# Windowed attention feeding a two-layer ELU network on one core: another order of the first weight and value loads, and of the last pair of the second tile

## The chip, the cores and the metric

The kernel runs on one core of one Trainium2 chip. The metric is the device time of one execution in microseconds. Three runs of the kernel before gave 301.75, 302.62 and 303.54 us; the median is 302.62 us.

## What is computed

There are 8 batches with 8 heads of 576 rows and 64 columns, so 4608 tokens of 512 values. Attention looks at a window of 32 rows on each side; its output goes through two dense layers with an ELU between them.

```python
# _attn_ref, for every batch and head
scores = 1/sqrt(D) * q @ k.T, kept where |i - j| <= 32
x = softmax(scores) @ v                      # [4608, 512] after the heads are put side by side
# _moe_ref
h = x @ w_in                                 # [4608, 2048]
g = np.where(h > 0.0, h, np.exp(np.minimum(h, 0.0)) - 1.0)
out = g @ w_out                              # [4608, 512]
```

Inputs and output are float32; inside the kernel the operands of the matmuls are bf16.

## The kernel before

**Attention by pairs.** A pair is two blocks of 64 query rows with all 8 heads, 128 tokens; there are 36. For pair i, `scores(i)` (L372) are 16 small matmuls into a PSUM tile, `exponential(i)` (L393) is one ScalarE instruction, `mask(i)` a VectorE product (pairs 0 to 3 get their band added in PSUM instead), `pv(i)` (L409) 16 matmuls against the values, `normalize(i)` (L423) a reciprocal and a product on VectorE that make `x_st`. `x_transpose(i)` (L434) turns `x_st` by four TensorE transposes into a PSUM bank, and `x_evac(i)` (L451) copies it into half of `xT[t]`, the moving operand of tile t. The PSUM tiles of pairs 2 and 3 are "s" and "u".

**Values in two layouts.** Even blocks read `V_e`, odd ones `V_o`, the same rows shifted by 64. For batch 0 the loads bring `V_o` (`load_v_odd`, L157), and `rotate_back` (L163) copies its halves into `V_e` on VectorE. `pv(3)` needs `load_v_odd(0, 3)` and half of the copy made from it.

**The dense layers by tiles and steps.** A tile is 256 tokens (two pairs); there are 18. A step is 256 columns of the middle layer, 8 for a tile. `mm1(kk)` (L703) is the first layer for step `order[kk]`: 8 matmuls of 256 columns for TensorE (`products`, L729), four for each half j of the step. Then comes `exponents(kk)` (L747), the exponential on ScalarE, and behind it `subtract(kk)` (L756), which takes 1 away, on ScalarE for kk 1, 3 and 4 and on VectorE otherwise. `elu(kk)` (L766) is one VectorE instruction that reads the PSUM tile and makes `g_sb`. `mm2(n)` (L820) adds step n to the output sums with 4 matmuls of 512 columns.

**The order of the start.** `order` begins with tile 0 steps 0 and 1 (kk 0, 1), tile 1 steps 0 and 1 (kk 2, 3), then tile 0 steps 2 and 3 (kk 4, 5), and so on. Steps kk 2 and 3 are made by pairs (`BY_PAIRS`, L727): first both with pair 2's 128 columns, then both with pair 3's, 8 matmuls of 128 columns each time, in the PSUM tiles "s" and "u". Every other `mm1` takes the tile "h0" or "h1", by the parity of kk, so `mm1(8)` waits until `elu(6)` has read "h0".

**What sets the order of the work.** The schedule is written out by hand: each engine runs its instructions in the order in which the program issues them. `at(kk, slot, fn, ...)` (L569) puts a call into step kk: "dve" ahead of `mm1`, "half" between the halves j of `mm1`, "mid" behind `mm1`, a number n ahead of `mm2(n)`, "end" at the end of the step. All loads with a cast to bf16 are issued on GpSimd's queue in program order (L488 to L502 and L547 to L557): values, weights, and the cast groups `load_cast` (L138) of queries and keys. `load_w_in(c, z, nz)` (L197) loads part z of nz of quarter c of w_in, which is two steps wide; half a quarter is one step, a quarter of it (a sixteenth of w_in) half a step. `load_w_out` (L205) does the same for the rows of w_out. The quarter 3 of w_in is first needed by `mm1(12)`.

**The cast groups.** `transpose_casts` (L595) runs `elu(8)`, then turns the queries and keys of batch 1's first part and of batch 0's last rows on TensorE: 38 transposes into two PSUM tiles, `pk` and `pt`. ScalarE evicts `pk`, VectorE `pt` with three copies. Pair 4 (`scores(4)` at the end of step 9) needs them, and takes the PSUM tile "s" that `pt` had.

Of the kernel before, what the change touches and what calls it, by code (L numbers as in the profile page):

```python
# [10 lines left out]
BF16 = mybir.dt.bfloat16  # L11
# [10 lines left out]
def kernel(  # L22
# [9 lines left out]
    nc = tc.nc  # L32
# [61 lines left out]
    def ps_tile(shape, dt, tag, name):  # L94
        return pools[tag].tile(shape, dt, tag=tag, name=name)
# [42 lines left out]
    def load_cast(b, which, part):  # L138
        z, nj = part
        mj = nj if nj < 3 else HJ + 1  # L140
        t = cpool.tile([128, 2, mj * D], BF16, tag=f"c{which}{mj}",
                       name=f"c{which}")[:, :, 0:nj * D]
        qk_c[b, which, z] = t
        src = (q, k)[which][b, :, z:z + NC * nj, :].rearrange(
            "(g h) (c j) d -> c g h (j d)", h=2, j=nj)
        nc.gpsimd.dma_start(out=t, in_=src)  # L146
# [10 lines left out]
    def load_v_odd(b, m):  # L157
        lo = 128 * m + WIN
        nc.gpsimd.dma_start(  # L159
            out=V_o[b % 3][:, m, :, 0:D],  # L160
            in_=v[b, :, lo:lo + 128, :].rearrange("h p d -> p h d"))

    def rotate_back(b, m0, m1, parts=(0, 1)):  # L163
        e, o = V_e[b % 3], V_o[b % 3]
        for z in parts:
            nc.vector.tensor_copy(e[64 * (1 - z):64 * (2 - z),
                                    m0 + z:m1 + z],
                                  o[64 * z:64 * (z + 1), m0:m1])
# [28 lines left out]
    def load_w_in(c, z=0, nz=1):  # L197
        w = D_FF // 4 // nz
        c = c * nz + z
        nc.gpsimd.dma_start(  # L200
            out=w_in_sb[:, :, c * w:(c + 1) * w],
            in_=moe_w_in[:, c * w:(c + 1) * w].rearrange(
                "(o p) f -> p o f", p=128))

    def load_w_out(c, z=0, nz=1):  # L205
        n = NFO // 4 // nz
        c = c * nz + z
        nc.gpsimd.dma_start(
            out=w_out_sb[:, c * n:(c + 1) * n, :],
            in_=moe_w_out[c * n * 128:(c + 1) * n * 128, :].rearrange(  # L210
                "(o p) f -> p o f", p=128))
# [51 lines left out]
    def make_masks():  # L263
        nc.gpsimd.affine_select(
            out=masks, in_=masks, compare_op=ALU.is_ge, fill=0.0,
            base=0, pattern=[[0, 5], [-1, QB]], channel_multiplier=1)
        nc.gpsimd.affine_select(
            out=masks, in_=masks, compare_op=ALU.is_ge, fill=0.0,
            base=2 * WIN, pattern=[[0, 5], [1, QB]], channel_multiplier=-1)
        for mi in (0, 4):  # L270
            nc.gpsimd.affine_select(
                out=masks[:, mi, :], in_=masks[:, mi, :],
                compare_op=ALU.is_ge, fill=0.0, base=-WIN,
                pattern=[[0, QB]], channel_multiplier=1)
        nc.gpsimd.affine_select(
            out=masks[:, 3, :], in_=masks[:, 3, :], compare_op=ALU.is_ge,
            fill=0.0, base=128 - WIN - 1, pattern=[[0, QB]],
            channel_multiplier=-1)
# [209 lines left out]
    for which in range(2):  # L488
        load_cast(0, which, FRONT_B[which])
    load_w_in(0, 0, 2)  # L490
    for m in (2, 3):
        load_v_odd(0, m)
    for z in (2, 3):
        load_w_in(0, z, 4)
    load_w_in(1)
    load_w_out(0, 0, 2)
    load_w_out(0, 1, 2)
    load_v(0, 4, HIGH)
    for which in range(2):
        load_cast(0, which, FRONT_C[which])  # L500
    load_w_out(1)
    make_masks()  # L502

    idle(10, "y1")
# [37 lines left out]
    scores(3)  # L542
    exponential(3)
    rotate_back(0, 2, 3)
    rotate_back(0, 3, 4, (0,))

    load_w_in(2, 0, 2)  # L547
    for which in range(2):
        load_cast(1, which, ONE_A)
    load_w_in(2, 1, 2)  # L550
# [18 lines left out]
    def at(kk, slot, fn, *args):  # L569
        tasks.setdefault((kk, slot), []).append((fn, args))  # L570

    def run(kk, slot):
        for fn, args in tasks.get((kk, slot), ()):
            fn(*args)
# [7 lines left out]
        at(kk + 2, "end", x_evac, i, nc.scalar)  # L582


    for i in (2, 3):
        at(0, ("half", "mid")[i - 2], pv, i)
        at(0, ("half", "mid")[i - 2], normalize, i)
    at(1, "half", x_transpose, 2, "y0")
    at(1, "half", x_evac, 2, nc.scalar)
    at(1, "mid", x_transpose, 3, "y1")  # L590
    at(1, "mid", x_evac, 3, nc.vector)
    at(5, "dve", swap_pools)


    def transpose_casts():  # L595
        elu(8)
        n, (nq, nk) = ONE_A[1], (c[1] for c in FRONT_C)
        pk = ps_tile([128, 1024], BF16, "h1", "ptx")
        pt = ps_tile([128, 2048], BF16, "s", "ptx")
        first, then = [], []  # L600
        transpose_qk(1, 1, ONE_A, 0, n, nc.scalar, later=first, pt=pk)
        for b, which, part, lo in ((1, 0, ONE_A, 0), (0, 0, FRONT_C[0], n),
                                   (0, 1, FRONT_C[1], n + nq)):
            transpose_qk(b, which, part, 0, part[1], nc.vector, later=then,
                         pt=pt[:, lo * 128:(lo + part[1]) * 128])
        for evict in first + then:
            evict()

    at(8, 6, transpose_casts)
    at(6, "dve", rotate_back, 0, 3, 4, (1,))  # L610

    for which in range(2):
# [18 lines left out]
    for i in range(4, NPAIR):  # L631
        two = i >= FIRST_TWO
        kk, z = begin[i], i % 2 if two else 0
# [69 lines left out]
    def mm1(kk):  # L703
        t, s = order[kk]
        if kk == BY_PAIRS[1]:
            return
        ks = BY_PAIRS if kk == BY_PAIRS[0] else (kk,)
        tags = ((f"h{kk % 2}", "s") if kk == NSTEP - 1 else
                ("s",) if kk == 2 else ("u",) if kk == 3 else (f"h{kk % 2}",))
        for k in ks:  # L710
            psH[k] = []
        for z, tag in enumerate(tags):
            for k in ks:
                psH[k].append(ps_tile([128, FG // len(tags), TT], FP32,
                                      tag if k == kk else "u", "ps"))
        for p in range(len(ks)):
            for k in ks:
                for z in range(len(tags)):
                    products(k, z, p if len(ks) > 1 else None)
                if p == len(ks) - 1:  # L720
                    for z in range(len(tags)):
                        exponents(k, z)
                        if k == NSTEP - 1:
                            elu(k, z)
# [4 lines left out]
    def products(kk, z, pair):  # L729
        t, s = order[kk]  # L730
        ps = psH[kk][z]
        w = ps.shape[1]
        for j in range(w):
            fo = s * FG + z * w + j
            for do in range(NDO):
                if pair is None:
                    o, r = ps[:, j, :], xT[t][:, :, do, :]
                else:
                    o = ps[:, j, pair * 128:(pair + 1) * 128]
                    r = xT[t][:, pair, do, :]  # L740
                nc.tensor.matmul(  # L741
                    o, lhsT=w_in_sb[:, do, fo * 128:(fo + 1) * 128],
                    rhs=r, start=(do == 0), stop=(do == NDO - 1))
            if j == 0 and pair is None:
                run(kk, "half")

    def exponents(kk, z):  # L747
        ps = psH[kk][z]
        e_sb = mpool.tile([128, ps.shape[1], TT], FP32, tag="e_sb",
                          name="e_sb")  # L750
        nc.scalar.activation(e_sb, ps, AX.Exp)  # L751
        e_t[kk, z] = e_sb
        if kk > 0:
            subtract(kk, z)
# [11 lines left out]
    def elu(kk, z=0):  # L766
        if z == 0:
            g_t[kk] = mpool.tile([128, FG, TT], BF16, tag="g_sb", name="g_sb",
                                   bufs=8)
        if kk == 0:  # L770
            subtract(kk, z)
        ps = psH[kk][z]
        w = ps.shape[1]
        nc.vector.scalar_tensor_tensor(  # L774
            g_t[kk][:, z * w:(z + 1) * w, :], ps, 0.0, m_t.pop((kk, z)),
            ALU.max, ALU.min)
# [70 lines left out]
    for kk in range(NSTEP):  # L847
        run(kk, "first")
        for n in {1: (), 2: (0, 1), 9: ()}.get(kk, (kk - 1,)):
            if n >= 0:  # L850
                elu(n)
        run(kk, "dve")
        mm1(kk)
        run(kk, "mid")
        if kk == NSTEP - 1:
            last_sums()
        elif kk >= LATE + LAG:
            for _ in range(3 if kk < LATE + LAG + 4 else 4):
                add(*todo.pop(0))
        else:  # L860
            for n in {2: (), 3: (), 4: (), 5: (0, 2), 6: (1, 3), 7: (4,),
                      8: (5, 6)}.get(kk, (kk - LAG,) if kk >= LAG else ()):
                run(kk, n)
                mm2(n)
        run(kk, "end")
# [30 lines left out]
```

## Time and profile before

| what | value |
|---|---|
| median of three runs | 302.62 us |
| the profiled execution's own time | 302.36 us |
| its span in the profile | 300.6 us |
| time around the span (302.36 - 300.6) | 1.76 us |
| TensorE (PE) busy | 293.7 us, 98% of the span |
| VectorE (DVE) busy | 242.1 us, 81% |
| ScalarE (ACT) busy | 169.0 us, 56% |
| GpSimd (POOL) busy | 52.3 us, 17% |
| granted TensorE clock | 1.0 |

Times in the profile count from the start of the span. In a line of the timeline the first number is the start, the second the length, both in us; what stands in brackets at the end is how long the engine had been idle and what ended that. Consecutive matmuls overlap in the records, so the distance between their starts, not their length, says what one costs. A load has a time of issue on its queue and a time to landing.

The loads at the start, all on GpSimd's queue, with the trace's own times:

| load | issued us | landed us |
|---|---|---|
| values for pair 2 (`load_v_odd(0, 2)`, 128 KB) | 7.15 | 14.60 |
| values for pair 3 (`load_v_odd(0, 3)`, 128 KB) | 8.02 | 15.56 |
| w_in third sixteenth (128 KB) | 8.88 | 17.00 |
| w_in fourth sixteenth (128 KB) | 9.63 | 17.40 |
| w_in quarter 1 (512 KB) | 10.41 | 19.92 |
| w_out, two halves of quarter 0 (256 KB each) | 11.14, 12.25 | 21.18, 23.03 |
| w_out quarter 1 (512 KB) | 17.29 | 26.26 |
| w_in, first half of quarter 2 (256 KB) | 19.79 | 27.60 |
| cast group of batch 1, queries and keys (256 KB each) | 20.55, 21.71 | 28.93, 30.20 |
| w_in, second half of quarter 2 (256 KB) | 23.32 | 31.50 |
| w_in quarter 3 (512 KB) | 27.89 | 38.95 |

### The profile page before, as it was taken

The page shows a single profiled execution, that of the slowest core. Times are in us where ns is not written, and L with a number is a line of the kernel's source. Part 1 is how long each engine was busy: PE and PEld are TensorE (multiplying, and loading weights), DVE is VectorE, ACT ScalarE, POOL GpSimd, SP SyncE. Part 2 cuts the span into 40 slices and gives each one's busy share as a digit, 9 for nine tenths or more (in the row PEclk, how much of TensorE's full clock was granted, in tenths as well). Part 3 has the DMA queues.
Part 4 walks back from the last instruction along what each step waited for, and adds up shares of the span by engine and source line. Part 5 has one row for each costly group of instructions (what it writes and reads, how often), then busy time and mean ns, then how long its engine had stood idle before and what let it go on. Part 6 is the DMA issues. An engine that isn't in the chain of part 4 may idle for free.

```text
span 300.6 us, 7712 instructions
## 1 busy us (share of the span) xinstructions
PE 293.7 (98%) x3116; PEld 198.1 (66%) x3116; DVE 242.1 (81%) x481; ACT 169.0 (56%) x256; POOL 52.3 (17%) x74
## 2 busy tenths in 40 slices
PE   6999999999999999999999999999999999999995
PEld 2575667677666666666666666666666666666673
DVE  6787787988787988887889789887988787877673
ACT  3873458688655567456745665467535353534332
POOL 8777204520005000410032002300000000000000
PEclk9999999999999999999999999999999999999999
DMA  9999999999967969999699989997921121111011
GB/s 190 167 198 202 187 232 338 372 190 171 290 181 209 234 115 260 236 280 140 158 264 326 161 203 253 310 155 141 271 47 72 35 72 38 70 37 70 2 70 71
DMA packets 94069, 52.74 MB, mean 175 GB/s; under 512 B 78162, under 2 KB 83794, under 8 KB 94034
## 3 DMA queue, kind: packets, MB, share of 16 engines
q0 software_dynamic: 44976, 10.03, 45.3%
q1 hardware_dynamic: 47330, 35.74, 44.7%
q10 hardware_dynamic: 1728, 6.49, 5.9%
q8 instruction: 24, 0.39, 0.6%
q14 instruction: 11, 0.09, 0.1%
HBM read 36.70 MB, written 15.34 MB: 173 GB/s over the span
## 4 chain that ended last, share of the span: by engine, by line
PE 90%; DMA 3%; POOL 3%; DVE 2%; ACT 1%; issue 1%; POOLq 0%; DVEq 0%; ACTq 0%
PE ps L741 41%; PE psY L794 40%; PE psS L417 3%; PE psS L385 3%; DMA w_in_sb<-in_moe_w_in_dram 3%; POOL Vo L159 1%; PE ptx L341 1%; PE psXT L439 1%; DVE g_sb L774 0%; POOL c L146 0%; ACT e_sb L751 0%; PE ptx L336 0%; DVE m_sb L763 0%; ACT pu L396 0%; ACT m_sb L761 0%
## 5 line engine op out<-in xcount | busy, mean ns | idle before, releaser
L751 ACT ACTIVATE e_sb<-ps 128x512 f32<-128x512 f32 (+1 forms) x145 | 86.1, 595 | 115.0 <-PE ps L741 108.9
L741 PE MATMUL ps<-xT,w_in_sb 128*128 128x256 bf16 (+1 forms) x1168 | 149.6, 272 | 0.5 <-DMA w_in_sb<-in_moe_w_in_dram 0.4
L794 PE MATMUL psY<-w_out_sb,g_sb 128*128 128x512 bf16 (+2 forms) x592 | 147.5, 374 | 0.0
L741 PEld LDWEIGHTS <-w_in_sb 128*128 128x128 bf16 x1168 | 110.5, 98 | 37.5 <-issue 0.7
L774 DVE SCALAR_TENSOR_TENSOR g_sb<-ps,m_sb 128x512 bf16<-128x512 f32 (+1 forms) x145 | 99.4, 686 | 13.2 <-DVE m_sb L763 0.5
L763 DVE TENSOR_SCALAR m_sb<-e_sb 128x512 bf16<-128x512 f32 (+1 forms) x142 | 60.9, 429 | 32.2 <-ACT e_sb L751 30.1
L794 PEld LDWEIGHTS <-g_sb 128*128 128x128 bf16 x592 | 55.9, 98 | 38.7
L152 POOL DMA_DIRECT2D Ve<-in_v_dram x37 | 32.2, 882 | 132.7 <-PE psS L417 79.6
L396 ACT ACTIVATE pu<-psS 128x1024 bf16<-128x1024 f32 x36 | 36.5, 1020 | 1.4 <-PE psS L385 1.4
L429 DVE TENSOR_TENSOR x_st<-psS,rc 128x512 bf16<-128x512 f32 x36 | 24.9, 692 | 1.2
L291 ACT CAST qkb<-f 128x768 bf16<-128x768 f32 (+2 forms) x29 | 25.1, 864 | 0.0
L405 DVE TENSOR_TENSOR pm<-pu,masks 128x1024 bf16<-128x1024 bf16 x32 | 21.8, 682 | 0.5 <-ACT pu L396 0.5
L417 PEld LDWEIGHTS <-pm 128*64 128x64 bf16 x512 | 9.7, 111 | 7.3 <-DVE pm L405 6.5
L293 DVE COPY y_sb<-psY 128x512 f32<-128x512 f32 (+1 forms) x18 | 12.2, 676 | 1.5 <-PE psY L794 1.5
L385 PEld LDWEIGHTS <-kT 64*128 64x128 bf16 x560 | 9.4, 95 | 4.6 <-issue 4.4
L291 ACT COPY y_sb<-psY 128x512 f32<-128x512 f32 (+1 forms) x19 | 10.8, 567 | 2.5 <-PE psY L794 2.5
L385 PE MATMUL psS<-qT,kT 64*128 64x64 bf16 x560 | 11.9, 191 | 0.1
L417 PE MATMUL psS<-Ve,pm 128*64 128x65 bf16 x288 | 11.6, 196 | 0.1
L417 PE MATMUL psS<-Vo,pm 128*64 128x65 bf16 x224 | 10.3, 197 | 0.0
L176 DVE COPY Vo<-Ve 64x1040 bf16<-64x1040 bf16 (+1 forms) x22 | 9.1, 413 | 0.7
L291 ACT COPY qT<-ptx 128x512 bf16<-128x512 bf16 (+4 forms) x7 | 6.3, 935 | 3.4 <-PE ptx L341 3.2
L293 DVE CAST qkb<-f 128x768 bf16<-128x768 f32 (+7 forms) x12 | 7.4, 642 | 0.2 <-DMA f<-in_q_dram 0.2
(55 smaller groups left out, 91.0 us busy)
## 6 DMA issues: line engine op xcount, KB each, us to landing
out_dram<-y_sb SPq DMA_DIRECT2D x36, 256.0 KB, 4.0
f<-in_q_dram SPq DMA_DIRECT2D x12, 576.0 KB, 5.8
f<-in_k_dram SPq DMA_DIRECT2D x12, 576.0 KB, 8.3
in_dram<-qkb ACTq DMA_DIRECT2D x10, 576.0 KB, 4.3
Ve<-in_v_dram POOLq DMA_DIRECT2D x21, 128.0 KB, 12.2
w_out_sb<-in_moe_w_out_dram POOLq DMA_DIRECT2D x3, 512.0 KB, 10.0
Ve<-in_v_dram POOLq DMA_DIRECT2D x14, 96.0 KB, 11.1
w_in_sb<-in_moe_w_in_dram POOLq DMA_DIRECT2D x2, 512.0 KB, 10.3
```

Of the source, the lines that this page charges most:

```text
L152: nc.gpsimd.dma_start(out=V_e[b % 3][p0:p1, m, :, 0:D], in_=v[b, :, lo + p0:lo + p1, :].rearrange("h p d -> p h d"))
L291: nc.scalar.copy(d_, s_)
L385: nc.tensor.matmul(psS[:, h % 2, hp * 128 + z * QB:hp * 128 + (z + 1) * QB], lhsT=keys, rhs=qT[b % 2][base:base + 64, hp, QB * qb:QB * (qb ...
L396: nc.scalar.activation(pu, _bap(psS, [psS.ap[0], [1, 1024]]), AX.Exp, scale=SCALE)
L405: nc.vector.tensor_mul(pm, pu, _bap(mm, [mm.ap[0], [0, H], [1, 2 * QB]]))
L417: nc.tensor.matmul(psS[QB * z:QB * (z + 1), par, hp * VD:(hp + 1) * VD], lhsT=pm[:, par * HP + hp, z * QB:(z + 1) * QB], rhs=vv[:, qb // 2 ...
L429: nc.vector.tensor_mul(x_st, _bap(psS, [psS.ap[0], [VD, HP], [512, 2], [1, D]]), _bap(rc, [rc.ap[0], [2, HP], [1, 2], [0, D]]))
L741: nc.tensor.matmul(o, lhsT=w_in_sb[:, do, fo * 128:(fo + 1) * 128], rhs=r, start=(do == 0), stop=(do == NDO - 1))
L751: nc.scalar.activation(e_sb, ps, AX.Exp)
L763: nc.vector.tensor_scalar(m_sb, e_sb, -1.0, None, ALU.add)
L774: nc.vector.scalar_tensor_tensor(g_t[kk][:, z * w:(z + 1) * w, :], ps, 0.0, m_t.pop((kk, z)), ALU.max, ALU.min)
L794: nc.tensor.matmul(sum_of(t, ts, c), lhsT=g_t[n][:, j, ts * 128:(ts + 1) * 128], rhs=w_out_sb[:, s * FG + j, cols_of(c)], start=(s == 0 an ...
```

## The change

The third sixteenth of w_in is issued ahead of pair 3's values, the fourth behind them. Quarter 1 of w_in is loaded in two halves. Quarter 1 of w_out is loaded in two halves too, and the first half of w_in's quarter 2 goes in between. In step 0 only `pv(2)` and `normalize(2)` are left. Pair 3's half copy, its `pv` and its `normalize` go into the middle of `mm1(1)`, behind pair 2's `x_transpose`. Pair 3's `x_transpose` goes behind the first 8 matmuls of `mm1(2)`, into a new slot "pair", and its `x_evac` from VectorE to ScalarE. `transpose_casts` goes from ahead of `mm2(6)` to behind it, and its tile `pk` from "h1" to "h0".

```diff
-    for m in (2, 3):
+    for m, z in ((2, 2), (3, 3)):
         load_v_odd(0, m)
-    for z in (2, 3):
         load_w_in(0, z, 4)
-    load_w_in(1)
+    load_w_in(1, 0, 2)
+    load_w_in(1, 1, 2)
...
-    load_w_out(1)
+    load_w_out(1, 0, 2)
     make_masks()
...
     rotate_back(0, 2, 3)
-    rotate_back(0, 3, 4, (0,))
 
     load_w_in(2, 0, 2)
+    load_w_out(1, 1, 2)
     for which in range(2):
         load_cast(1, which, ONE_A)
...
-    for i in (2, 3):
-        at(0, ("half", "mid")[i - 2], pv, i)
-        at(0, ("half", "mid")[i - 2], normalize, i)
+    at(0, "half", pv, 2)
+    at(0, "half", normalize, 2)
     at(1, "half", x_transpose, 2, "y0")
     at(1, "half", x_evac, 2, nc.scalar)
-    at(1, "mid", x_transpose, 3, "y1")
-    at(1, "mid", x_evac, 3, nc.vector)
+    at(1, "half", rotate_back, 0, 3, 4, (0,))
+    at(1, "half", pv, 3)
+    at(1, "half", normalize, 3)
+    at(2, "pair", x_transpose, 3, "y1")
+    at(2, "pair", x_evac, 3, nc.scalar)
...
-        pk = ps_tile([128, 1024], BF16, "h1", "ptx")
+        pk = ps_tile([128, 1024], BF16, "h0", "ptx")
...
-    at(8, 6, transpose_casts)
+    at(8, "end", transpose_casts)
...
                 for z in range(len(tags)):
                     products(k, z, p if len(ks) > 1 else None)
+                if p == 0:
+                    run(k, "pair")
                 if p == len(ks) - 1:
```

## The prediction

> **What bounds the kernel now.** I read the page first: engine shares, then the chain that ended last.
>
> ```profile
> PE 293.7 (98%) x3116; PEld 198.1 (66%) x3116; DVE 242.1 (81%) x481; ACT 169.0 (56%) x256; POOL 52.3 (17%) x74
> ...
> PE 90%; DMA 3%; POOL 3%; DVE 2%; ACT 1%; issue 1%; POOLq 0%; DVEq 0%; ACTq 0%
> ```
>
> TensorE is busy 98%, and 90% of the chain is its own matmuls. So an edit counts only where it lengthens or fills a gap of TensorE, and the edits all lie ahead of 40 us. Second, the waits of PE from 13 us to the end:
>
> ```profile
> PE ps L741 <- DMA w_in_sb<-in_moe_w_in_dram: 0.4, 1, 0.4
> PE ps L741 <- DVE g_sb L774: 0.2, 1, 0.2
> ```
>
> These are all: 0.6 us of idle. Third, the chain in order of time shows what stands between the two (start, length, what):
>
> ```profile
> 8.88 8.11 DMA w_in_sb<-in_moe_w_in_dram
> 17.00 0.05 issue
> 17.05 0.61 PE ps L741 x4
> ...
> 18.55 1.52 PE ps L741 x24
> ...
> 20.09 0.02 ACT e_sb L751
> ...
> 22.36 0.64 ACT m_sb L761
> ...
> 23.02 0.04 DVE g_sb L774
> ...
> 28.49 1.03 PE ps L741 x8
> ```
>
> mm1(1) waits for the third sixteenth of w_in (landed 17.00). From 18.55 on the chain is the third block of 8 half-width matmuls, then ScalarE without a pause, then VectorE without a pause until elu(6) frees "h0" for mm1(8) at 28.49. So what delays that third block arrives whole at 28.49; TensorE's own work there would have been ready 0.34 us earlier (last mm2 start 27.93, spacing 0.216, hence 28.15), which a later block shifts too. Fourth, the timeline of PE round 18 us, and that of ACT below it (start, length, engine, line, operation):
>
> ```profile
> 17.49 0.39 PE L439 MATMUL psXT<-ident,x_st 128*128 128x128 bf16 x4
> 17.71 0.60 PE L741 MATMUL ps<-xT,w_in_sb 128*128 128x256 bf16 x4
> 18.15 0.39 PE L439 MATMUL psXT<-ident,x_st 128*128 128x128 bf16 x4
> ```
>
> ```profile
> 17.91 0.58 ACT L291 COPY xT<-psXT 128x512 bf16<-128x512 bf16 x1 [0.97 <-PE psXT L439]
> 18.40 0.60 ACT L751 ACTIVATE e_sb<-ps 128x512 f32<-128x512 f32 x1
> 19.03 0.63 ACT L761 ACTIVATE m_sb<-e_sb 128x512 bf16<-128x512 f32 x1
> ```
>
> Pair 3's transpose runs at 18.15 and VectorE copies it at 18.58 to 19.00, well ahead of its use by the third block at 19.44 (18.55 plus 16 spacings of 0.0555). ScalarE meanwhile does e(1) and m(1), until 19.66.
>
> **What the Trainium skill says.** "TensorE: Matmul & The Clock Gate", Step-by-step, has matmuls stay in program order, only weight loads being pulled ahead. The trace agrees: pair 2's x_st was written by 16.84, its transpose ran at 17.49, behind the matmul that waited. The same page, Back-to-back issue gap, gives 262 cycles for 256 columns; the trace has 0.109 us a matmul (17.05 to 17.49 for four). "DMA: Bandwidth & Descriptors", Two DMAs through the same engine are not ordered, has descriptors of one queue start in order; GpSimd's loads landed in the order of issue throughout. The same page, Why small descriptors are slow, gives each packet a fixed overhead; in the trace 512 KB of w_in took 2.52 and 1.92 us between landings, 256 KB pieces 1.30 to 1.53.
>
> **The change, part by part.**
>
> *Loads.* Between the landing of pair 2's values (14.60) and the fourth sixteenth (17.40) lie 2.80 us for one 128 KB value load and two sixteenths. The gaps are 0.96 for the values, 1.44 and 0.40 for the sixteenths. With the order turned I put the third sixteenth at 14.60 + 1.3 = 15.9 (bounds 15.3 and 16.1, from a mean sixteenth, 0.92, to the larger gap), pair 3's values at 15.9 + 0.9 = 16.8 (bounds 16.3 and 17.4: its own gap after the earliest; together with the fourth sixteenth) and the fourth at 17.45.
>
> *The stall that goes.* mm1(0) ends its matmuls at 15.71 + 0.44 = 16.15, so mm1(1)'s first half can start there, 0.9 us earlier. Late next is VectorE: pv(2)'s last matmul ends at 15.77; reciprocal and product follow (16.83 to 17.76 for pair 3, 0.93), so x_st is ready at 16.75. TensorE waits from 16.59 to 16.80 for it, and transposes until 17.02.
>
> *Pair 3's values.* The half copy takes 0.29 (15.59 to 15.88) and starts at the later of 16.78 (VectorE free) and 16.85 (landed): to 17.14. pv(3), 0.39 of matmuls, starts at 17.19, and mm1(1)'s second half at 17.6 (the fourth sixteenth is there by 17.5). Its last matmul ends at 17.6 + 0.33 + 0.27 = 18.20. Behind the waiting pv(3) stand all later matmuls.
>
> *x of pair 3.* pv(3) ends at 17.65, its normalize at 18.63; the transposes run at 18.68 between the first two half-width blocks, which need "s" and "u" free (16.75, 18.63) and have cover enough. Their copy is now on ScalarE, in order behind e(1) and m(1): e(1) at 18.25, m(1) at 18.88 (0.63 later, as before), the copy 0.54 later, at 19.42, for 0.58: 20.00. The third block can start at 20.04 instead of 19.44: **+0.60**. VectorE is spared 0.42 us, but it isn't late here; its gap ahead of 23.02, 0.46, waits for ScalarE. By the chain above +0.60 reaches mm1(8). Below nothing this can't go while the copy is behind m(1): if pv(3) waits for VectorE alone it is still +0.54.
>
> *Cast group.* In front of the transposes TensorE now has mm2(6) too, and `pk` needs "h0", which elu(8) must have read. Before, mm1(8) started at 28.49 and elu(8) ended at 31.41 (30.72 + 0.69): 2.92 later. mm1(8) (0.873) and two mm2 (0.864 each) cover 2.60. So the transposes start 2.97 after mm1(8) instead of 2.69 without that wait (the change of shape costs 0.09, by 30.32 against 30.22): **+0.28**. Bounds: 0 if elu(8) comes 0.3 sooner; 0.5 if VectorE is late. The copies of `pt` end 1.86 after the transposes (31.50 to 33.36), and scores(4), which needs them, now comes after mm1(9) and mm2(7), 1.83: **+0.08**. From there pv(4) waits for ScalarE and VectorE as before. The landing of the keys, 30.20, has 1.8 us of room here.
>
> *Splits and swaps.* w_in's quarter 1 in halves costs the DMA queue 2 x 1.30 - 2.52 = 0.1 to 2 x 1.53 - 2.52 = 0.5 us. w_out's rows keep their length: nothing. GpSimd issues two loads more, 0.75 each, ahead of loads that are 8 to 11 us from landing; the masks, ready at 19.8, are first used at 35.78. Every landing after it is later by 0.1 to 0.5, covered by 0.9 us at w_out's first half (21.18; used 22.08) and more elsewhere, but for one: w_in's quarter 3 landed at 38.95, and mm1(12) started at 38.99, where its weight load came 0.22 after the one before it instead of 0.11. So TensorE already waits there by **0.12**, which a later TensorE gets back.
>
> *Sum.* 0.60 + 0.28 + 0.08 - 0.12 = 0.84. After 40 us TensorE runs as before. 302.36 + 0.84 = **303.2 us**; the profiled execution is 0.26 under the median of 302.62, so I would as soon see 303.5. The clock row shows 9 in all slices, across a start distance of 0.55 at 17.05 as well, so I charge nothing for a lower clock.
>
> **Rivals.**
>
> *The wait is only exchanged.* If the copy on ScalarE cost nothing, the third block could start at 16.15 + 4 x 0.44 + 2 x 0.22 + 0.39 = 18.74, 0.7 early, which pays for the cast group's 0.36. But mm1(12) can't start before w_in's quarter 3, 0.1 to 0.5 later than before, mean 0.3: 302.36 + 0.3 = 302.7. For it: the stall is the page's longest. Against it: ScalarE's order.
>
> *Slower: pair 3's values come late.* Behind a sixteenth of longer packets they could land with the fourth, or after it: both sixteenths needed 1.84 together after values before. Each 0.1 us past 16.85 is 0.1 on pv(3), hence on e(1), the copy and all else. At 17.8, the total is 0.84 + 0.95 = 1.8: 304.2. It passes the 0.5% mark (1.5 us) from a landing at 17.5. Against it: value loads took 0.84 to 1.25 after each other.
>
> *The change doesn't do what it says:* the third sixteenth lands at 17.0 all the same (its old gap plus the swap of issue hidden). Then mm1(1)'s first half starts at 17.05, pv(3) follows at 17.7, the second half at 18.1, the third block at 20.55: 1.1 + 0.24 = 1.35, 303.7.
>
> **How the numbers follow.** Forecast 0.57 (its own range 302.8 to 303.8), exchange 0.13, late values 0.15, no earlier weights 0.10, a gain that none of these mechanisms gives 0.05. An end-to-end measurement tells some 0.5% (1.5 us, by the runs' 301.75 to 303.54) from no change. Slower by more: the late values and a part of the forecast's and the third rival's upper ends, 0.24. Faster by more needs a gain beyond all gaps seen ahead of 40 us: 0.04. Within: 0.72. The range 302.3 to 304.6 leaves out the gain and the tail of the late values.
>
> **What would show it.** Right: no wait for w_in at mm1(1); a new wait of the third half-width block for ScalarE's copy, with the block at about 20.0; mm1(8) at about 29.1; the cast transposes waiting for elu(8) by some 0.3; mm1(12) without a wait for its load; the end of the span near 301.4. Wrong: the block ahead of 19.5, pair 3's values past 17.4, or a load that TensorE waits for after 25 us.

## The result, and the profile after

The changed kernel's median over 22 runs is 303.16 us (302.68 to 304.95), against 302.45 us (301.64 to 303.54) for the kernel before. The ratio is 1.0035 with a 95% interval of 1.0023 to 1.0047, so 1.06 us more (0.7 to 1.4). That is the distance of the averages (303.43 and 302.38); the medians differ by 0.71, because the changed kernel has more long runs. The forecast was 0.84 more. Here and below a ratio leaves out single runs over 1.5% longer than the fastest of their kernel, while the medians are over all runs. The profiled execution took 303.60 us with a span of 301.9; it lies 0.4 above the median, and carries one wait that not every execution has (below).

The page of the changed kernel, the lines that answer to those of before (TensorE has 52 records fewer here, which are missing ones, so its busy share can't be compared):

```profile
PE 291.3 (96%) x3064; PEld 198.4 (66%) x3116; DVE 241.7 (80%) x480; ACT 169.6 (56%) x257; POOL 53.4 (18%) x76
...
PE 84%; DMA 5%; DVE 3%; POOL 3%; issue 2%; ACT 2%; POOLq 0%; DVEq 0%; SPq 0%; ACTq 0%
```

TensorE's share of the chain fell from 90 to 84%; other engines and DMA gained what it lost. Its waits from 13 us to the end (waiting engine, tile and line, what ended the wait, us in total, times, longest):

```profile
PE ptx L341 <- ACT xT L291: 0.5, 1, 0.5
PE ptx L336 <- DVE g_sb L778: 0.4, 1, 0.4
PE ps L745 <- ACT xT L291: 0.4, 1, 0.4
PE psS L417 <- DVE Ve L166: 0.3, 1, 0.3
PE psY L798 <- issue: 0.3, 2, 0.2
PE psS L385 <- DVE kT L293: 0.2, 1, 0.2
```

The wait for w_in at mm1(1) is gone, and so is the one for elu(6) at mm1(8). In their place stand pv(3) waiting for the half copy of its values (L417), the third half-width block waiting for pair 3's x (L745), the cast group waiting for elu(8) (L336), scores(4) waiting for pt's copies (L385), and one that the prediction did not have, 0.5 at L341. The chain in order of time shows the first of them:

```profile
8.76 8.15 DMA Vo<-in_v_dram
16.91 0.02 issue
16.93 0.30 DVE Ve L166
17.23 0.04 issue
17.27 0.45 PE psS L417 x16
17.72 0.56 PE ps L745 x4
18.28 0.02 issue
18.30 0.61 ACT e_sb L755
18.91 0.02 issue
18.93 0.63 ACT m_sb L765
19.56 0.48 ACT xT L291
20.05 0.04 issue
20.09 2.80 PE ps L745 x32
```

From the landing of pair 3's values at 16.91 the chain goes without slack through the half copy, pv(3), the second half of mm1(1), e(1), m(1) and the copy of x to the third block at 20.09 (19.44 before).

One table serves for what follows. Times are from one profiled execution of each kernel, in us after that execution's own mm1(0) (14.4 to 15.1), since the start differs by up to 0.7 from execution to execution. It is no effect of the change: it lies at 14.44 to 15.10 in the eight kernels with the new order of the first loads, at 14.69 to 14.82 in the six with the old one. In the changed kernel's profile it is 0.35 earlier than in the one before, so a time read from the start of the span flatters the change by that. A step's start is that of its second weight load. The last two columns are absolute. e1 to e12 are the experiments.

| kernel | pair 3's values landed | third block | mm1(8) | mm1(8) to mm1(9) | mm1(12), absolute | w_in's quarter 3 landed, absolute |
|---|---|---|---|---|---|---|
| before | 0.77 | 4.65 | 13.70 | 3.88 | 39.01 | 38.95 |
| changed | 2.47 | 5.65 | 14.35 | 4.18 | 39.55 | 39.10 |
| e1 copy ahead | 2.08 | 5.09 | 13.88 | 4.17 | 40.00 | 39.94 |
| e2 casts early | 2.40 | 5.58 | 14.28 | 3.89 | 40.12 | 40.07 |
| e3 both | 1.10 | 5.60 | 14.36 | 3.89 | 39.83 | 38.30 |
| e4 casts late alone | 0.21 | 4.23 | 12.94 | 4.17 | 38.38 | 38.06 |
| e5 loads alone | 2.45 | 5.75 | 14.45 | 3.89 | 39.51 | 39.45 |
| e6 pair 3 alone | 1.10 | 5.25 | 14.19 | 3.88 | 39.55 | 37.96 |
| e7 no splits | 1.11 | 5.25 | 13.95 | 4.18 | 39.80 | 38.97 |
| e8 gate early | 0.94 | 5.25 | 13.95 | 4.17 | 39.15 | 38.48 |
| e9 splits alone | 0.55 | 4.23 | 13.00 | 3.89 | 39.29 | 39.24 |
| e10 w_in halves | 0.53 | 4.50 | 13.25 | 3.89 | 39.21 | 39.15 |
| e11 w_out halves | 0.18 | 4.33 | 13.03 | 3.89 | 38.50 | 38.44 |
| e12 w_in ahead | 0.63 | 4.23 | 13.29 | 3.89 | 38.46 | 36.91 |

### The profile page after: what moved, and what is told of

Its sections match the earlier page's. It is cut to its first block, busy times and chain, and to the rows that moved or that the text cites. A ratio compares the mean times of both kernels' runs of the same rounds, so it can differ in the third digit from the quotient of the medians.

```text
span 301.9 us, 7663 instructions
## 1 busy us (share of the span) xinstructions
PE 291.3 (96%) x3064; PEld 198.4 (66%) x3116; DVE 241.7 (80%) x480; ACT 169.6 (56%) x257; POOL 53.4 (18%) x76
## 4 chain that ended last, share of the span: by engine, by line
PE 84%; DMA 5%; DVE 3%; POOL 3%; issue 2%; ACT 2%; POOLq 0%; DVEq 0%; SPq 0%; ACTq 0%
PE ps L745 39%; PE psY L798 38%; PE psS L417 3%; PE psS L385 3%; DMA Vo<-in_v_dram 3%; DMA f<-in_q_dram 2%; ACT e_sb L755 1%; PE ptx L341 1%; POOL Vo L159 1%; DVE g_sb L778 1%; DVE m_sb L767 1%; DVE qT L293 1%; POOL w_in_sb L200 0%; POOL c L146 0%; PE ptx L336 0%
## 5 line engine op out<-in xcount | busy, mean ns | idle before, releaser
L745 PE MATMUL ps<-xT,w_in_sb 128*128 128x256 bf16 (+1 forms) x1168 | 149.6, 271 | 0.4 <-ACT xT L291 0.4
L798 PE MATMUL psY<-w_out_sb,g_sb 128*128 128x512 bf16 (+2 forms) x541 | 139.0, 373 | 2.8 <-issue 0.3
L745 PEld LDWEIGHTS <-w_in_sb 128*128 128x128 bf16 x1168 | 110.6, 98 | 36.9 <-issue 0.7
L767 DVE TENSOR_SCALAR m_sb<-e_sb 128x512 bf16<-128x512 f32 (+1 forms) x142 | 61.7, 434 | 32.7 <-ACT e_sb L755 30.6
L417 PEld LDWEIGHTS <-pm 128*64 128x64 bf16 x512 | 9.6, 110 | 7.3 <-DVE pm L405 6.5
L385 PEld LDWEIGHTS <-kT 64*128 64x128 bf16 x560 | 9.5, 95 | 4.9 <-issue 4.0
L385 PE MATMUL psS<-qT,kT 64*128 64x64 bf16 x560 | 11.9, 191 | 0.5 <-DVE kT L293 0.2
L417 PE MATMUL psS<-Ve,pm 128*64 128x65 bf16 x288 | 11.5, 196 | 0.1
L417 PE MATMUL psS<-Vo,pm 128*64 128x65 bf16 x224 | 10.3, 196 | 0.0
L426 DVE RECIPROCAL rc<-psS 128x8 f32<-128x8 f32 x36 | 7.2, 199 | 1.9 <-PE psS L417 1.7
```

The costliest lines, as they stand in the source:

```text
L385: nc.tensor.matmul(psS[:, h % 2, hp * 128 + z * QB:hp * 128 + (z + 1) * QB], lhsT=keys, rhs=qT[b % 2][base:base + 64, hp, QB * qb:QB * (qb ...
L417: nc.tensor.matmul(psS[QB * z:QB * (z + 1), par, hp * VD:(hp + 1) * VD], lhsT=pm[:, par * HP + hp, z * QB:(z + 1) * QB], rhs=vv[:, qb // 2 ...
L745: nc.tensor.matmul(o, lhsT=w_in_sb[:, do, fo * 128:(fo + 1) * 128], rhs=r, start=(do == 0), stop=(do == NDO - 1))
L767: nc.vector.tensor_scalar(m_sb, e_sb, -1.0, None, ALU.add)
L798: nc.tensor.matmul(sum_of(t, ts, c), lhsT=g_t[n][:, j, ts * 128:(ts + 1) * 128], rhs=w_out_sb[:, s * FG + j, cols_of(c)], start=(s == 0 an ...
```

## The experiments

My theory after the result: three parts cost, pair 3's chain, the cast group's two waits, and later landings after the splits. The rivals: all of it is ScalarE's order (the prediction's step), or all of it is the loads.

**e1, the copy of pair 3's x ahead of m(1).**

```diff
     at(2, "pair", x_evac, 3, nc.scalar)
+    at(2, "pair", lambda: subtract(1, 0))
+    at(2, "pair", lambda: elu(1))
...
-        if kk > 0:
+        if kk > 1:
             subtract(kk, z)
...
-        for n in {1: (), 2: (0, 1), 9: ()}.get(kk, (kk - 1,)):
+        for n in {1: (), 2: (0,), 9: ()}.get(kk, (kk - 1,)):
```

> The changed kernel with pair 3's x copy on ScalarE ahead of m(1); elu(1) goes behind it. If ScalarE's order is what made the third half-width block late (the prediction's step), the copy follows e(1) at once, the block starts 0.6 us earlier against its own mm1(0), and the time falls by 0.3 to 0.6 us, ratio to before about 1.0015 to 1.0025. If the chain of pair 3 itself is late (values landed 16.91, half copy, pv, normalize, transposes end 19.2 in the changed kernel's profile), the copy can move from 19.47 to 19.25 only: block 0.2 earlier, time down by 0.0 to 0.2, ratio 1.003 to 1.0035.

Measured: 303.33 us, ratio 1.0036 (1.002 to 1.0051): no gain is seen, though with intervals of this width one of some 0.5 us can't be excluded. The same holds for every comparison of e1, e2, e3 and e7 with the changed kernel (1.0023 to 1.0047): no difference there is clear of the noise, and the traces carry the argument. ScalarE's timeline in the changed kernel and then in e1 (start, length, engine, line, operation, and how long it had been idle for what):

```profile
18.30 0.60 ACT L755 ACTIVATE e_sb<-ps 128x512 f32<-128x512 f32 x1 [0.74 <-PE ps L745]
18.93 0.63 ACT L765 ACTIVATE m_sb<-e_sb 128x512 bf16<-128x512 f32 x1
19.47 0.57 ACT L291 COPY xT<-psXT 128x512 bf16<-128x512 bf16 x1
```

```profile
18.10 0.60 ACT L757 ACTIVATE e_sb<-ps 128x512 f32<-128x512 f32 x1 [0.35 <-PE ps L747]
19.07 0.58 ACT L291 COPY xT<-psXT 128x512 bf16<-128x512 bf16 x1 [0.38 <-PE psXT L439]
19.55 0.63 ACT L767 ACTIVATE m_sb<-e_sb 128x512 bf16<-128x512 f32 x1
```

With m(1) out of its way the copy waits for the transposes instead. From the landing of pair 3's values the third block comes after 3.01 us (19.71 - 16.70) against 3.18 in the changed kernel (20.09 - 16.91): ScalarE's order is worth 0.17 there, not 0.6. Against its own mm1(0) e1's block is 0.56 earlier, nearly what the first theory asks for, but 0.39 of that is the earlier landing of the values. The other kernels agree: from the start of the half copy to the third block it is 3.16 or 3.17 in the changed kernel, e2, e6, e7 and e8, whether the values landed 2.4 or 1.0 after mm1(0), and 2.98 in e1. The rest is pair 3's own chain. The profile of e1 also shows why even that did not reach the end: w_in's quarter 3 landed at 39.94, and TensorE waited for it.

```profile
PE ps L747 <- DMA w_in_sb<-in_moe_w_in_dram: 0.6, 1, 0.6
PE ps L747 <- ACT xT L291: 0.2, 1, 0.2
PE ptx L336 <- DVE g_sb L780: 0.2, 1, 0.2
```

**e2, the cast group back at its place; e3, e1 and e2 together; e4, the cast group's move alone, on the kernel before.** e2 is this edit, e4 its reverse:

```diff
-        pk = ps_tile([128, 1024], BF16, "h0", "ptx")
+        pk = ps_tile([128, 1024], BF16, "h1", "ptx")
...
-    at(8, "end", transpose_casts)
+    at(8, 6, transpose_casts)
```

> The changed kernel with the cast group back ahead of mm2(6) and pk back in h1. If the wait for elu(8) and for pt's copies is a cost of this part alone, mm1(9) comes 3.88 us after mm1(8) instead of 4.17 and scores(4) 1.83 after mm1(9) instead of 1.91: 0.36 less at pair 4, of which w_in's quarter 3 may take back 0.1: time down by 0.25 to 0.36, ratio 1.0023 to 1.0027. If the wait only moves to another place (a late landing of the keys, mm1(12)'s weights), no change: 1.0035.

> Both edits above together. If their costs add: down by 0.3 to 0.55 us, ratio 1.0017 to 1.0025. If w_in's quarter 3 (landed 39.10 in the changed kernel) is then the bound at mm1(12), the sum is cut: the PE waits for it there, and the ratio isn't under 1.001. A ratio under 0.998 would speak for a part of the change that gains, which I don't expect.

> The kernel before with the cast group moved behind mm2(6) and pk in h0, nothing else. If this part's cost is the prediction's (0.28 for elu(8), 0.08 for pt's copies, 0.12 got back at mm1(12)): up by 0.24 us, ratio 1.0008, mm1(9) 4.15 after mm1(8), no wait left at mm1(12). If elu(8) is read in time: mm1(9) 3.88 after mm1(8), ratio 1.000.

Measured: e2 303.07 us, 1.0026 (1.0014 to 1.0038); e3 303.14, 1.0028 (1.0016 to 1.004); e4 302.47, 1.0006 (0.9993 to 1.0018). TensorE's transposes of the cast group, in the kernel before (where mm1(8) started at 28.49) and in the changed one (28.79):

```profile
30.32 1.25 PE L336 MATMUL ptx<-ident,c 128*64 128x128 bf16 x38
```

```profile
31.77 1.25 PE L336 MATMUL ptx<-ident,c 128*64 128x128 bf16 x38 [0.44 <-DVE g_sb L778]
```

The distance from mm1(8) to mm1(9) is 4.17 or 4.18 in every kernel with the group behind mm2(6), whatever else is in it, and 3.88 or 3.89 in every kernel with it ahead: 0.29, forecast 0.28. mm1(10) follows mm1(9) by 2.25 against 2.18: 0.07, forecast 0.08. e4's ratio stands for 0.2 us (-0.2 to 0.5), which agrees with the forecast's 0.24 and doesn't by itself exclude none. e3 shows no more gain than e2: in its profile the half copy of pair 3's values took 0.84 us, not 0.29 (last section), and the third block was as late as in the changed kernel. From the start of that copy it came after 3.52, which is e1's 2.98 and the 0.55 that the copy was longer.

**e5, the new order of loads alone; e6, pair 3's part alone.** e5 is the diff's edits of the loads on the kernel before. e6 is the third sixteenth ahead of pair 3's values with the diff's edits of pair 3, on the kernel before; w_in's and w_out's quarters stay whole and the cast group stays early.

> The kernel before with the new order of loads alone (third sixteenth ahead of pair 3's values, w_in's and w_out's quarter 1 in halves, w_in's quarter 2 between). pv(3) stays ahead of mm1(1). If pair 3's values, now landing about 1.3 us later than before, are what costs: pv(3) waits for them at about 17.3 and mm1(1) behind it, the wait for w_in at mm1(1) is gone, the third half-width block is 0.4 to 0.6 later, time up by 0.3 to 0.7 us, ratio 1.001 to 1.0025. If only the new place of pair 3's work costs, the loads alone gain the stall of 0.4 us or change nothing: ratio 0.999 to 1.000.

> The kernel before with the third sixteenth ahead of pair 3's values and pair 3's work in its new place; the other loads and the cast group as before. If pair 3 is the main cost: third half-width block 0.6 later as in the changed kernel, mm1(8) 0.3 later, no wait at mm1(12): time up by 0.2 to 0.5, ratio 1.001 to 1.002. If the whole 1.0035 comes from later landings after the splits, this one is at 1.000.

Measured: e5 302.67 us, 1.0008 (0.9991 to 1.0024); e6 302.76, 1.0005 (0.9992 to 1.0018). Neither interval excludes none. The traces are clearer than the times. In e5 TensorE waits 1.3 us for the half copy of pair 3's values, because pv(3) still stands ahead of mm1(1):

```profile
PE psS L417 <- DVE Ve L166: 1.3, 1, 1.3
```

Its third block is at 5.75. The changed kernel, with pair 3's work moved and the values as late (2.47 against 2.45), has it at 5.65: at such a landing the move saves 0.10. With the values 1.3 to 1.5 earlier (e6, e7, e8) the block is at 5.25. Then VectorE, not the landing, sets the start of the half copy (2.08 after mm1(0) in all three), and the chain of 3.17 follows. But the kernel before has the block at 4.65, and the five experiments that keep the old order of these four loads (e4, e9 to e12) at 4.23 to 4.50. Even with values on time and ScalarE's order of e1 it would be at 2.08 + 2.98 = 5.06, an estimate. From mm1(0) to mm1(12) the eight kernels with the new order take 24.58 to 25.59, the six with the old one 23.68 to 24.50. e6's TensorE is 0.3 to 1.2 us behind all of these at mm1(12), its measured time 0.15 us (-0.2 to 0.5); single executions differ by that much, so the size of this part stays open between 0 and 0.5.

**e7, the changed kernel without the splits.**

```diff
-    load_w_in(1, 0, 2)
-    load_w_in(1, 1, 2)
+    load_w_in(1)
...
-    load_w_out(1, 0, 2)
+    load_w_out(1)
...
-    load_w_out(1, 1, 2)
```

> The changed kernel with w_in's and w_out's quarter 1 whole, in one load each at the old place. The first part of batch 1's second half of queries landed at 46.44 in the changed kernel's profile against 44.80 before, and its cast on ScalarE made TensorE wait 0.5 to 0.7 us at 48. If the splits make that landing late: w_in's quarter 3 lands 0.1 to 0.5 earlier, no wait at 48, time down by 0.3 to 0.7, ratio 1.001 to 1.0025. If the lateness is of that one execution (the spread of its 22 times reaches from 302.7 to 304.9), no change within 0.1%.

Measured: 303.04 us, 1.0022 (1.0001 to 1.0043), and no wait of TensorE for a late load or for ScalarE's cast of one. The interval holds 1.0035 too. What the splits touch shows in the changed kernel at 46 us. Batch 1's second part of queries landed at 46.44 (44.80 in the profile before), and ScalarE's cast of it stands ahead of a copy of x. The cast before, and then the changed kernel's lines:

```profile
44.98 1.25 ACT L291 CAST qkb<-f 128x1280 bf16<-128x1280 f32 x1
```

```profile
45.03 0.60 ACT L755 ACTIVATE e_sb<-ps 128x512 f32<-128x512 f32 x1 [1.63 <-PE ps L745]
46.52 1.26 ACT L291 CAST qkb<-f 128x1280 bf16<-128x1280 f32 x1 [0.89 <-DMA f<-in_q_dram]
47.68 0.58 ACT L291 COPY xT<-psXT 128x512 bf16<-128x512 bf16 x1
```

The 0.89 of ScalarE becomes the 0.5 of TensorE at L341 in the list of waits; from mm1(12) to mm1(17) the changed kernel takes 11.61 us, the kernel before, e1, e2, e3, e6 and e7 10.96. e4, without a split, has 11.35 there, and e5, with them, 11.18; in both ScalarE waited for the same landing (0.63 and 0.46). So this wait comes and goes with the execution. In e1 and e2 TensorE had already waited about as long at mm1(12), for w_in's quarter 3 (0.6 and 0.8).

**e8, the loads of batch 1's second half released earlier.**

```diff
-    gate(w_in_at(3))
+    gate(V_e[1][64:65, 2, 0, 0:1])
```

> The changed kernel with the loads of batch 1's second half released by the landing of batch 1's third value load (about 37.1) instead of w_in's quarter 3 (39.1). If the wait at 48 is for these loads: the cast on ScalarE starts without a wait for them, TensorE has no wait at 48, and both median and spread fall: ratio 1.001 to 1.0025. If they take bandwidth from w_in's quarter 3 or w_out's quarter 3 (needed at 39.5 and about 44), a wait comes there and the time is the same or longer.

Measured: ten runs, from 303.02 to 314.03 us. Six of them, up to 306.25, give the ratio 1.0067 (1.0032 to 1.0102); the other four took 312.00 to 314.03, and the profile is of the longest. The first theory missed; the second had the sign, not the place. The chain has one piece that shows where this execution lost its time:

```profile
30.99 26.98 DMA Ve<-in_v_dram
```

The last values of batch 1, issued on GpSimd's queue at 30.05 and 30.99, landed at 49.10 and 57.97, after 19 and 27 us instead of the 13 and 12 of the changed kernel. From 40 to 60 us SP's queue, with the loads released early, moved 6.29 MB and GpSimd's 0.14:

```profile
q1 hardware_dynamic: 1874, 6.29, 84.2%
q0 software_dynamic: 1051, 0.14, 10.6%
```

VectorE then waits for these values, and TensorE for VectorE (4.6 and 3.9 us). In that execution the gate on w_in's quarter 3 would have guarded the values behind it too. Whether the six shorter runs are longer than the changed kernel for the same reason isn't shown.

**e9, the splits alone; e10, w_in's halves alone; e11, w_out's halves alone (with w_in's quarter 2 between); all on the kernel before.**

> The kernel before with w_in's and w_out's quarter 1 in halves and w_in's quarter 2 between the halves; nothing else. The changed kernel without the splits was at 1.0022, with them at 1.0035, and the two parts without splits (pair 3, cast group) at 1.0005 and 1.0006. If the splits delay w_in's quarter 3 and the queries of batch 1, which TensorE and ScalarE wait for: w_in's quarter 3 lands later by 0.3 to 1.0, time up by 0.3 to 0.6 us, ratio 1.001 to 1.002. If the splits are covered, as the prediction had it: ratio 1.000 within 0.0012.

> The kernel before with only w_in's quarter 1 in halves (rows of 256 columns instead of 512). If shorter rows are what delays the queue: about all of the cost of e9, 1.001 to 1.002. If the number of loads or the order is: half of it or less, 1.000 to 1.001.

> The kernel before with only w_out's quarter 1 in halves and w_in's quarter 2 between them (rows as long as before). Shorter rows as the cause: 1.000. The place of the masks and of the second half on GpSimd's queue, or the loads' number, as the cause: 1.001 or more.

Measured: 302.68 us, 1.0008 (0.9997 to 1.002); 302.39, 0.9999 (0.9988 to 1.001); 302.50, 1.0002 (0.9991 to 1.0012). So neither kind of halves alone shows a cost, to within 1.001 for w_in's and 1.0012 for w_out's. On the queue w_in's two halves took 2.39 to 2.73 us (2.58 on average over eight kernels), the whole quarter 2.18 to 2.54 (2.41 over six): 0.17 more, inside the prediction's 0.1 to 0.5. In the profiles of e9 and e10 TensorE waits 0.9 and 0.6 us for w_in's quarter 3, in e11 under 0.3 (2.22 from mm1(11) to mm1(12) instead of 1.96). The line of e9:

```profile
PE ps L743 <- DMA w_in_sb<-in_moe_w_in_dram: 0.9, 1, 0.9
```

That load landed at 38.30 to 40.07, on average 39.32, in the seven kernels with w_in's halves (changed, e1, e2, e3, e5, e9, e10; e8 apart), and at 37.96 to 38.97, on average 38.48, in before, e4, e6, e7 and e11. With e8, whose later loads start sooner, the first average is 39.22. The averages differ by 0.84 (0.73 with e8), where the prediction had 0.1 to 0.5 for this landing; but single executions spread by 1.0 to 1.8 within each group, so the split's own share in it stays open.

**e12, w_in's quarter 3 ahead of the third value load of batch 1, on the kernel before.**

```diff
-    for m in range(3):
+    for m in range(2):
         load_v(1, m)
     load_w_in(3)
+    load_v(1, 2)
```

> The kernel before with w_in's quarter 3 ahead of the third value load of batch 1. If mm1(12) waits for w_in's quarter 3 in many executions (0.12 us in the profiled one, 0.6 to 0.8 where it landed at 40): that load lands 0.9 earlier, the wait is gone and the time falls by 0.1 to 0.3, ratio 0.999 to 0.9997, unless the values (then about 38.9, copied from at about 40) are late instead: 1.000 or more.

Measured: 302.24 us, 1.0003 (0.9985 to 1.0022). The load landed at 36.91 and the wait is gone, but mm1(12) is at 38.46, where e4 has it (38.38) with the load at 38.06: with the load this early, TensorE's own work is the bound. No version here is clearly faster than the kernel before.

## Why the prediction was right, point by point

**The size and sign** held: 0.84 forecast, 1.06 (0.7 to 1.4) measured. The three parts alone add to 1.0006 + 1.0005 + 1.0008, so 0.0019, with about 0.002 of uncertainty; the whole is 0.0035. Whether the parts cost more together than alone is not settled.

**"The stall that goes"** went, but was worth less than the profile before showed. There mm1(1) began 2.26 after mm1(0). In e4, e9, e10, e11 and e12, with the same order of these loads and the same work, it began 1.84 to 1.94 after it, and the third block 0.15 to 0.42 earlier. In these five executions the old order had little of this stall to give.

**The loads.** Pair 3's values were put at 16.8 (bounds 16.3 to 17.4) and landed at 16.91; over the eight kernels with the new order it was 15.39 to 17.10, so the upper bound held everywhere and the lower failed in four. The third sixteenth was put at 15.9, not under 15.3, and landed at 14.36: 0.57 after the load ahead of it, not 1.3. Then the values took 2.55, not 0.9. So 16.91 against 16.8 is luck: two misses that cancelled. The wide gap (1.44 before, 2.55 for the values after) is not the sixteenth's: it turns up at another load in other executions. e4 has the old order, and its two sixteenths came after 0.40 and 1.52 where before had 1.44 and 0.40.

**"x of pair 3"** was reckoned well step by step: e(1) was put at 18.25, m(1) at 18.88, the copy at 19.42 and the block at 20.04, and they came at 18.30, 18.93, 19.47 and 20.09. But +0.65 by the clock of the span is +1.00 from mm1(0), because that start came 0.35 earlier; with the values early (e6, e7, e8) it is +0.60. The rivals' text names ScalarE's order as what stands against a gain, and supposes a third block at 18.74 without it. That is the step that failed in its reason: e1 gives the order 0.17, and the remainder belongs to half copy, pv, normalize and transposes in a row, which start later than before.

**"By the chain above +0.60 reaches mm1(8)"** failed: of the block's delay 0.35 was lost on the way. By the clock of the span mm1(8) is at 28.79 against 28.49, +0.30; from mm1(0) it is +0.65, near the forecast, but only because the block itself was 1.00 late. TensorE's own work was the bound (28.15 + 0.65), VectorE no longer. Its timeline before, and then in the changed kernel:

```profile
23.63 0.67 DVE L763 TENSOR_SCALAR m_sb<-e_sb 128x512 bf16<-128x512 f32 x1
24.40 0.69 DVE L774 SCALAR_TENSOR_TENSOR g_sb<-ps,m_sb 128x512 bf16<-128x512 f32 x1
25.12 0.58 DVE L166 COPY Ve<-Vo 64x520 bf16<-64x520 bf16 x1
```

```profile
24.27 0.42 DVE L767 TENSOR_SCALAR m_sb<-e_sb 128x512 bf16<-128x512 f32 x1
24.79 0.69 DVE L778 SCALAR_TENSOR_TENSOR g_sb<-ps,m_sb 128x512 bf16<-128x512 f32 x1
25.51 0.38 DVE L166 COPY Ve<-Vo 64x520 bf16<-64x520 bf16 x1
```

The same two instructions took 0.67 and 0.58 before, 0.42 and 0.38 after: the chain that looked packed was long only because of how long these instructions happened to take. From the third block to mm1(8) TensorE needs 8.70 us, the least seen: the changed kernel, e2, e4, e5, e7, e8 and e11 take it, with this half copy at 0.29 to 0.42. With the copy at 0.54 to 0.56, in e1, e3, e9 and e10, it is 8.75 to 8.80; with 0.74 and 0.71, in e6 and e12, 8.94 and 9.06. Before has 9.05.

**"Cast group"** held to 0.01: 0.29 and 0.07 (0.28 and 0.08).

**"Already waits there by 0.12"** at mm1(12) held in the changed kernel's profile, where TensorE came 0.45 after the landing. Its other half, that the landings after the splits are covered, held there but not in e1, e2, e9 and e10 (0.6 to 0.9 of waiting).

**What the sum lacked** is the cast at 46 us. The profiled execution is 1.25 longer in span: it starts mm1(0) 0.35 earlier, needs 0.89 more from there to mm1(12), then 0.65 for that cast and 0.06 behind it. The 0.89 stands beside the forecast's 0.84, with 0.65 to mm1(8), 0.36 for the cast group and 0.12 got back; but in it a block that was 0.40 later than forecast and the 0.35 lost before mm1(8) offset each other, which is luck. The 0.65 is not in the forecast, and no rival had it. It doesn't come in every execution, so its share in the measured 1.06 stays open.

**The rivals.** Late values were priced rightly in kind: in the changed kernel and e2 they landed 2.4 after mm1(0) instead of the 1.1 of e6 and e7, which moves the third block by 0.3 to 0.4. "The change doesn't do what it says" did not happen: the third sixteenth landed at 14.34 to 15.16 in all eight kernels with the new order, not at 17.0. "The wait is only exchanged" had its floor at mm1(12) right, as e1 and e2 show, but supposed a third block 0.7 early, which no kernel had.

## What to carry to other kernels

A stall for a load, read from one execution, is a draw: before paying for its removal, see how far the landings move between executions, here by 1 us and more over 15 us of queue. When work is moved behind a late landing, follow the whole chain of that work to its consumer (load, copy, matmul, normalize, transpose, copy) and not only the last engine in it. And where TensorE is full, price the waits by distances inside one execution, step to step: 0.29 was visible there in every trace with the group moved, while the timed ratio of that part alone had an interval of 0.7 us.

## What the runs showed of the hardware

**VectorE beside GpSimd.** The half copy of pair 3's values took 0.29 us in the other thirteen profiles and 0.84 in e3. There GpSimd was issuing loads (16.48 to 17.88 without a pause); VectorE in e3, then GpSimd in e3:

```profile
17.17 0.84 DVE L166 COPY Ve<-Vo 64x520 bf16<-64x520 bf16 x1
```

```profile
16.48 0.71 POOL L146 DMA_DIRECT2D c<-in_k_dram  x1 [0.33 <-DMA Vo<-in_v_dram]
17.18 0.70 POOL L208 DMA_DIRECT2D w_out_sb<-in_moe_w_out_dram  x1
```

The m_sb instruction (128x512 from float32) took 0.40 to 0.43 where no GpSimd instruction ran beside it in the two main profiles, and up to 0.72 beside one, though often 0.43 there as well. The Trainium skill has this in "SBUF — State Buffer", Who interferes with whom: a copy or tensor_scalar in VectorE's two-port modes and a GpSimd instruction exclude each other. The traces agree in part: the slow ones all ran beside a GpSimd instruction, but the half copy at 14.95 in the profile before, wholly inside one, took 0.29. Which instruction is hit differs from execution to execution.

**One queue held up by another.** In e8's profiled execution GpSimd's loads of 128 and 96 KB took 19 and 27 us to land beside SP's, whose packets are larger (6.29 MB in 1874 packets against 0.14 MB in 1051). The Trainium skill's "DMA: Bandwidth & Descriptors", Queues, rings and completion order, has the engines take turns between queues by packets. That SP's queue had 84.2% of the engines' time and GpSimd's 10.6% fits its direction; but the packets were not one for one, and their size was not varied, so the rule itself isn't shown here.
